# Block-sparse attention and a GELU layer: the selection masks of two more head pairs transposed by DMA

## The chip, the cores and the metric

The kernel runs on one core of a Trainium2 chip. The metric is the device time of one execution in microseconds (us). Times are medians of several runs; the profile shows one execution in detail. The core has a matrix engine (TensorE, PE in the profile, with its weight loads as PEld), a vector engine (VectorE, DVE), a scalar engine (ScalarE, ACT), a general engine (GpSimd, POOL) and SyncE (SP), whose queue issues almost all transfers here. Each engine works through its own instructions in order and waits on semaphores for the others. Transfers run on 16 shared DMA engines.

## The reference

Input q, k and v have 4 batches, 8 heads, 768 positions and 64 columns per head. Keys are averaged over blocks of 64 positions, each query scores the 12 averages, and may look at its three best blocks (among those not in its future) and at its own block. Attention over the allowed, causal positions follows, and its result, 3072 rows of 512, goes through a two-layer network with 2048 inner columns and the tanh form of GELU.

```python
gate_scores = np.einsum('bhsd,bhnd->bhsn', q, k_rep)
gate_scores = np.where(causal, gate_scores, -1000000000.0)
top_idx = np.argsort(gate_scores, axis=-1)[..., -top_k:]
...
scores = np.where(mask, scores, -1000000000.0)
attn = np.exp(scores)
attn = attn / (np.sum(attn, axis=-1, keepdims=True) + 1e-09)
...
h = x @ w_in
g = 0.5 * h * (1.0 + np.tanh(c * (h + 0.044715 * h * h * h)))
return (g @ w_out).astype(np.float32)
```

## The kernel before, in words

Heads are worked on in pairs, 16 in all: pairs 0 to 3 are batch 0 and have steps of their own, pairs 4 to 15 share one set of steps. The whole program is a list of steps, the string ORDER, written out by a planner; `do` takes them one after the other, so an engine's own sequence is the sequence of that engine's steps in the list. A step's name is a letter or two, the pair, and sometimes a part; behind `:` stands the engine that a copy runs on (a ScalarE, v VectorE, p GpSimd), behind `@` which of three PSUM slots ("wide" tiles, two banks each) a product uses.

For a pair p of 4 to 15, in rough order: `d` loads q, k and v (two transfers each, line 422). `hn` and `ln` split q and k into a high and a low 16-bit part (lines 184, 186, 738). `zqh`, `zkh` and `zql` turn them by a DMA transpose on SP (line 750), and `c0`, `c1` copy the halves into the operand tile `qk` (line 757). `s` and `b` make the block sums of the keys on PE (`kp`, line 764) and VectorE, `g` the gate scores on PE (line 793). `m` selects on VectorE: eight-largest search, comparison, and at line 820 the mask `madd16`, laid out by query.

The score product wants the mask by block, as 12 additional rows of `qk` beside the 64 rows of q. So the mask is transposed, and this is where there are two ways. `mt` (line 829) does five 128x128 transposes on PE into the PSUM tile "small", of which there is one for all users: `kp`, `gt`, `mt` and `xt` take it in turn. `zm` (line 839) does one DMA transpose on SP into an SBUF tile that shares two buffers with `zql`. Pairs 4 to 12 use the first, pairs 13 to 15 the second. Either way `mc` (line 845) then copies the two heads' 12 rows into `qk`, on the engine that ORDER names.

`k` are six groups of score products into wide tiles (`st`, line 858), `x` their exponentials on ScalarE (line 874), `a` the causal cut on GpSimd (line 888), `p` the weighted sums of v (`pv`, line 900), `n` the division by the sum on VectorE (lines 672 and 676). `xt`/`xc` (PE and a copy) or `zx` (a DMA transpose, line 909) put the result into `xT`. Batch 0's steps of the same letters have the lines 477, 511, 634 and 661.

The two-layer network runs in 12 chunks of 256 rows, woven between the pairs: `u` are the products with w_in into a wide tile (`hps`, line 966, eight products of 256 columns in each half), `y` the GELU on ScalarE (line 976), `f` the products with w_out (line 1002), `o` the copy to SBUF (line 1015), `w` the store (line 1020). The weights are loaded by `lw` (line 344) into seven buffers shared with other tiles (`w32`) and converted by `cw` (line 353). `dm` are products of zeros that keep PE running in its early waits (line 1041).

Around the change the list holds, for pair 11, `u.4.3.1 mt.11.0 y.5.3`, then `u.4.2.0`, the VectorE copy `mc.11.0.1`, `hn1.12.0`, the ScalarE copy `mc.11.0.0`, `ln1.12.0`; for pair 12, `p.10.0.1 x.11.0.4 mt.12.0 k.11.0.2 mc.12.0.0`, and later `n.10.0` and `mc.12.0.1`, both copies on VectorE.

Of the kernel before, what the change touches and what calls it, by code (L numbers as in the profile page):

```python
# [39 lines left out]
a.1.1.0 xt.1.0 v.0.1.0:a k.0.1.0.1@1 k.0.1.1.1@2 ma.0.1.1 lw.in.3 x.0.1.1.1 xc.1.0:v lw.in.2  # L40
k.0.1.0.0@0 xt.0.0 xc.0.0:v x.0.1.0.1 k.0.1.1.0@2 ma.0.1.0 dm5 cw.in.1:p x.0.1.0.0 u.0.3.0@1
u.0.3.1 r.0.2.0:p x.0.1.1.0 v.0.1.1:v a.0.1.1 a.0.1.0 r.0.2.1:v cw.in.0:v lw.out.1 lw.out.4
d0.0.4.2 r.1.2.0:p d.4.0 p.1.1.0@0 p.1.1.3 p.1.1.1 p.1.1.2 u.0.2.0@2 n.1.1 u.0.2.1 lw.out.0 y.0.3
xt.1.1 p.0.1.0@0 xc.1.1:v p.0.1.2 p.0.1.1 y.0.2 p.0.1.3 u.0.0.0@1 n.0.1 cw.in.2:a d.4.1 u.0.0.1
r.1.2.1:v cw.in.3:a xt.0.1 t2.0.2@2 xc.0.1:v y.0.0 u.1.2.0@0 hn0.4.0:p s.0.2 u.1.2.1 b.0.2 h2.0.2
t2.1.2@1 y.1.2 l.0.2 cw.out.0:p g.0.2 u.1.1.0@0 lw.out.2 cw.out.1:p m.0.2 lw.out.3 u.1.1.1 lw.out.5
d.5.0 s.1.2 cw.out.4:p mt.0.2 u.1.0.0@2 y.1.1 mc.0.2:v lw.out.7 lw.out.6 ln0.4.0:v u.1.0.1 h2.1.2
cw.out.2:v u.0.1.0@0 y.1.0 l.1.2 d.5.1 u.0.1.1 hn1.4.0:v cw.out.3:v u.1.3.0@2 b.1.2 y.0.1 ln1.4.0:v
u.1.3.1 hn0.5.0:p cw.out.5:v k.0.2.0.0@1 y.1.3 zql.4.0 k.0.2.1.0@0 ma.0.2.0 g.1.2 f.0.0.0 m.1.2
x.0.2.0.0 cw.out.6:p k.0.2.0.1@2 f.0.0.1 s.4.0 x.0.2.1.0 k.0.2.1.1@1 b.4.0 zqh.4.0 ma.0.2.1  # L50
ln0.5.0:v mt.1.2 f.0.0.2 x.0.2.1.1 c.ke.0.1:v d0.0.5.2 k.0.2.0.2@0 x.0.2.0.1 k.0.2.1.2@1 cw.out.7:v
ma.0.2.2 d.6.0 hn1.5.0:v x.0.2.1.2 mc.1.2:a k.1.2.1.0@2 zql.5.0 a.0.2.1 x.0.2.0.2 k.1.2.0.0@1
ma.1.2.0 f.0.0.3 c.q0.0 x.1.2.0.0 c0.4.0.1:v a.0.2.0 d0.1.4.2 g.4.0 o.0.0:a v.0.2.0:p x.1.2.1.0
k.1.2.0.2@0 zkh.4.0 m.4.0 k.1.2.1.2@1 ma.1.2.2 f.0.1.0 v.0.2.1:a x.1.2.0.2 d0.1.5.2 p.0.2.0@2
p.0.2.3 ln1.5.0:v p.0.2.2 c0.4.0.0:a mt.4.0 hn0.6.0:v x.1.2.1.2 d.6.1 ln0.6.0:v p.0.2.1 mc.4.0.0:a
k.1.2.1.1@0 v.1.2.0:p n.0.2 k.1.2.0.1@1 zqh.5.0 mc.4.0.1:a ma.1.2.1 f.0.1.1 c.ke.0.0:a c1.4.0.0:p
c.par.1 zkh.5.0 xt.0.2 x.1.2.0.1 c1.4.0.1:p f.0.1.2 xc.0.2:v c.ke.1.0:v c.q0.1 x.1.2.1.1 s.5.0
# [1035 lines left out]
```

## Time and profile before

| what | value |
|---|---|
| median of 3 runs | 269.88 us |
| the runs | 269.58, 269.88, 270.49 us |
| the profiled execution | 269.6 us, of which the profile's span is 267.9 us |
| instructions in the span | 6830 |
| mask transposes on PE (line 829) | 45, in nine pairs |
| mask transposes by DMA (line 839) | 3 |
| packets under 512 bytes | 105008 of 116431 |

The profile is a page and a set of views of one execution, with times counted from the start of the span. A view of the order of time gives the start of an instruction, how long it took, its engine, its line, what it writes and reads, and how many like it follow; in brackets stands the idle time of its engine before it and what ended that. A view of one tile gives all that writes or reads it, with the shortest, median and longest duration. For SP the time of a transfer is that of its issue; how long it took until the data had landed is a line of its own. Matmuls are pipelined, so their durations overlap; the distance between two starts tells what one costs.

### The profile page before, as it was taken

The numbers are of one execution on the slowest core, as the hardware profiler recorded it, in microseconds if no ns is written. First come the engines' busy times: TensorE is split into PE (matmuls) and PEld (weight loads), VectorE is DVE, ScalarE is ACT, GpSimd is POOL, SyncE is SP. The second block draws the span as 40 slices with busy tenths as digits, with TensorE's granted clock in tenths as the row PEclk, the third lists the DMA queues.
The fourth block names the chain that finished last, engine by engine and source line by source line (L and its number), as shares of the span: only waits on it lengthen the run. The fifth ranks groups of instructions, "written<-read, shape, count | busy, mean of one in ns | idle before, by whom it ended". The sixth has DMA issues, their size and how long they took to land.

```text
span 267.9 us, 6830 instructions
## 1 busy us (share of the span) xinstructions
PE 257.9 (96%) x2756; PEld 179.8 (67%) x2756; DVE 140.9 (53%) x441; ACT 194.5 (73%) x221; POOL 98.9 (37%) x166
## 2 busy tenths in 40 slices
PE   8778999999999999999999999999999999999994
PEld 4545898456668667977676656968666877795641
DVE  3667579788878786657564467523633120011111
ACT  2866966999899987949996968889999924351200
POOL 8375553346506737631874153005332200000000
PEclk9999999999999999999999999999999999999999
DMA  8999999999899996898998995397140400031212
GB/s 159 291 302 336 360 269 336 173 192 232 180 190 177 214 187 163 153 231 167 160 184 173 208 183 121 56 167 174 37 113 17 100 0 2 0 117 63 106 69 78
DMA packets 116431, 43.14 MB, mean 161 GB/s; under 512 B 105008, under 2 KB 109360, under 8 KB 116400
## 3 DMA queue, kind: packets, MB, share of 16 engines
q1 hardware_dynamic: 114288, 42.19, 72.3%
q10 hardware_dynamic: 2112, 0.52, 1.1%
q8 instruction: 21, 0.34, 0.6%
q14 instruction: 10, 0.08, 0.1%
HBM read 27.26 MB, written 6.29 MB: 125 GB/s over the span
## 4 chain that ended last, share of the span: by engine, by line
PE 91%; ACT 5%; DVE 2%; issue 1%; POOL 0%; ACTq 0%; DVEq 0%; POOLq 0%
PE hps L966 31%; PE ops L1002 27%; PE st L858 10%; PE pv L900 6%; PE pso L1002 4%; ACT at L634 3%; PE dm L1041 2%; PE w L463 2%; PE pv L661 1%; PE kp L764 1%; PE st L597 1%; PE st L615 1%; PE gt L793 1%; ACT qk L469 1%; PE mt L829 1%
## 5 line engine op out<-in xcount | busy, mean ns | idle before, releaser
L966 PE MATMUL hps<-xT,w_in 128*128 128x256 f16 x768 | 89.9, 272 | 0.0
L1002 PE MATMUL ops<-w_out,gT 128*128 128x512 f16 (+1 forms) x352 | 82.9, 372 | 0.0
L966 PEld LDWEIGHTS <-w_in 128*128 128x128 f16 x768 | 73.9, 98 | 11.6
L976 ACT ACTIVATE gT<-hps 128x1024 f16<-128x1024 f32 x48 | 48.1, 1024 | 37.2 <-PE hps L966 34.6
L874 ACT ACTIVATE at<-st 128x1024 f16<-128x1024 f32 (+1 forms) x72 | 63.0, 917 | 8.6 <-PE st L858 7.6
L1002 PEld LDWEIGHTS <-gT 128*128 128x128 f16 x400 | 37.3, 97 | 37.0 <-issue 0.8
L888 POOL TENSOR_SCALAR_AFFINE_SELECT at<-at 128x256 f16<-128x256 f16 x72 | 30.7, 445 | 76.1 <-ACT at L874 75.8
L858 PE MATMUL st<-qk 76*128 76x128 f16 (+2 forms) x192 | 36.6, 305 | 0.0
L738 DVE SCALAR_TENSOR_TENSOR ln<-io,hn 128x768 f16<-128x768 f32 x24 | 25.9, 1084 | 8.0 <-ACT hn L184 5.7
L634 ACT ACTIVATE at<-st 128x768 f16<-128x768 f32 (+1 forms) x24 | 20.9, 918 | 3.2 <-PE st L615 3.0
L858 PEld LDWEIGHTS <-qk 76*128 76x128 f16 x192 | 16.4, 97 | 9.5 <-issue 0.4
L186 POOL TENSOR_SCALAR hn<-io 128x768 f16<-128x768 f32 x8 | 17.3, 2162 | 10.2 <-DMA io<-in_q_dram 10.1
L1015 DVE COPY osb<-ops 128x512 f32<-128x512 f32 (+1 forms) x11 | 7.2, 652 | 23.4 <-PE ops L1002 23.4
L900 PEld LDWEIGHTS <-at 128*128 128x128 f16 x504 | 17.0, 97 | 1.2
L900 PE MATMUL pv<-v,at 128*128 128x65 f16 x504 | 17.7, 193 | 0.0
L757 POOL COPY qk<-khT 64x768 f16<-64x768 f16 x13 | 13.9, 1074 | 5.7 <-DMA khT<-hn 3.4
L976 ACT ACT_TABLE_LOAD x10 | 12.8, 1283 | 0.2
L1015 DVE COPY w_o<-ops 128x512 f32<-128x512 f32 x3 | 2.1, 692 | 20.1 <-PE ops L1002 20.1
L676 DVE TENSOR_TENSOR xn<-pv,zrec 128x768 f16<-128x768 f32 x12 | 11.5, 958 | 0.4
L672 DVE RECIPROCAL zrec<-pv 128x12 f32<-128x12 f32 x12 | 2.8, 230 | 16.1 <-PE pv L900 16.0
L1015 ACT COPY osb<-ops 128x512 f32<-128x512 f32 x5 | 2.9, 586 | 11.2 <-PE ops L1002 11.2
L1041 PE MATMUL dm<-zsrc 128*128 128x512 f16 (+3 forms) x31 | 9.8, 437 | 1.1 <-POOL zsrc L234 1.1
(150 smaller groups left out, 308.8 us busy)
## 6 DMA issues: line engine op xcount, KB each, us to landing
io<-in_q_dram SPq DMA_DIRECT2D x24, 192.0 KB, 4.4
io<-in_k_dram SPq DMA_DIRECT2D x24, 192.0 KB, 3.8
w_in<-in_moe_w_in_dram SPq DMA_DIRECT2D x8, 512.0 KB, 6.9
w_out<-in_moe_w_out_dram SPq DMA_DIRECT2D x8, 512.0 KB, 7.1
out_dram<-osb SPq DMA_DIRECT2D x15, 256.0 KB, 2.8
w_v<-in_v_dram SPq DMA_DIRECT2D x16, 192.0 KB, 4.2
out_dram<-w_o SPq DMA_DIRECT2D x8, 256.0 KB, 2.2
io<-in_v_dram SPq DMA_DIRECT2D x12, 128.0 KB, 5.7
```

The lines of the kernel that those rows point to most:

```text
L186: math_on[eng].tensor_scalar(out=out, in0=in_, scalar1=c, scalar2=None, op0=ALU.mult)
L634: nc.scalar.activation(out=ov, in_=iv, func=AF.Exp, bias=0.0, scale=SCALE / (QS * QS))
L738: math_on[eng].scalar_tensor_tensor(out=g.rearrange("p t c -> p (t c)"), in0=IO[p, x].rearrange("p t h d -> p (t h d)"), scalar=QS, in1=U[ ...
L757: copy_on[eng](out=dst[0:64, :], in_=U["qh" if x == 0 else "kh", p][64 * hh:64 * hh + 64])
L858: nc.tensor.matmul(st[:, hh, cb:cb + nq * 128], kt[p % 2][hh][0:64 + NBLK, jc * 128:(jc + 1) * 128], qt[p % 2][hh][0:64 + NBLK, qc * 128:( ...
L874: nc.scalar.activation(out=ov, in_=iv, func=AF.Exp, bias=0.0, scale=SCALE / (QS * QS))
L888: nc.gpsimd.affine_select(out=a, in_=a, compare_op=ALU.is_ge, fill=0.0, base=0, pattern=[[0, 2], [1, 128]], channel_multiplier=-1,)
L900: nc.tensor.matmul(U["pv", p][:, o:o + 65], AT[p, hh, jc, qc], v16[p % NSLOT][:, jc, hh, :], start=(jc == 0), stop=(jc == qc),)
L966: nc.tensor.matmul(hps[:, j * TCH:(j + 1) * TCH], w_in16[:, ci, fi * 128:(fi + 1) * 128], xT[:, ci, t0:t0 + TCH], start=(ci == 0), stop=(c ...
L976: nc.scalar.activation(out=g.rearrange("p a w -> p (a w)"), in_=G["h", ch, dj], func=AF.Gelu_apprx_tanh, bias=0.0, scale=1.0,)
L1002: nc.tensor.matmul(G["o", ch, ti][:, a:b], G["g", ch, dj][:, j, row * 128:(row + 1) * 128], w_out16[:, fi, a:b], start=(fi == 0), stop=(fi ...
L1041: nc.tensor.matmul(U["dm"][:, 0:m * 128].rearrange("p (a x) -> p a x", a=m), zsrc, zsrc.unsqueeze(1).to_broadcast([128, m, 128]), start=Tr ...
```

## The change

Two conditions change: pairs 11 and 12 get the step `zm` in place of `mt`. And ORDER is written anew. Taken engine by engine, its sequences are those of before with these exceptions: PE no longer has `mt.11.0` and `mt.12.0`; SP has `zm.11.0` between `w.3.0` and `zkh.12.0`, and `zm.12.0` between `d.15.0` and `zkh.13.0`; on VectorE `mc.11.0.1` comes after `ln1.12.0` and `mc.12.0.0` after `n.10.0`; on ScalarE `mc.11.0.0` comes after `y.4.2`. How the steps of different engines are interleaved in the list differs from the first line on, the wide slots 0 and 1 are exchanged from there on (with `p.1.0.0` and `k.1.1.1.1` taking each the other's slot), and the shared `w32` buffers are asked for by `lw.out.1`, `lw.out.4` and `r.0.2.0`, and by `d.10.2` and `o.3.1`, in another order.

```diff
-        if p in (13, 14, 15):
+        if p in (11, 12, 13, 14, 15):
             step(f"zm.{un}", mask_dma, p)
         else:
             step(f"mt.{un}", mask_t, p)
```

The lines of ORDER around the two masks and the slot exchange:

```diff
-x.1.1.1.0 l.0.1 b.0.1 p.1.0.0@0 p.1.0.1 p.1.0.3 p.1.0.2 x.1.1.0.0 v.0.0.0:v k.1.1.1.1@1 cw.in.4:p
...
-g.11.0 f.4.0.0 w.3.0 m.11.0 x.10.0.2 a.10.0.3 u.4.3.0@0 a.9.0.4 hn1.13.0:p u.4.3.1 mt.11.0 y.5.3
-u.4.2.0@2 mc.11.0.1:v a.9.0.3 hn1.12.0:v u.4.2.1 a.9.0.0 mc.11.0.0:a ln1.12.0:v zkh.12.0 v.10.0:p
...
-p.10.0.1 x.11.0.4 mt.12.0 k.11.0.2@2 mc.12.0.0:v a.11.0.4 f.5.0.0 x.11.0.2 n.10.0 c1.12.0.1:p
-f.5.0.1 a.11.0.5 zx.10.0 mc.12.0.1:v c1.12.0.0:p k.11.0.3@1 ln1.13.0:v f.5.0.2 x.11.0.3 d.14.1
...
+dd.1.2.0 b.0.1 cw.in.4:p x.1.1.0.0 lw.in.1 p.1.0.0@1 p.1.0.1 p.1.0.3 p.1.0.2 lw.in.0 k.1.1.1.1@0
...
+u.4.3.1 zm.11.0 y.5.3 u.4.2.0@2 a.9.0.3 hn1.12.0:v u.4.2.1 a.9.0.0 ln1.12.0:v zkh.12.0 v.10.0:p
+y.4.3 u.5.1.0@0 y.4.2 p.9.0.0@1 d.14.0 v.11.0:p u.5.1.1 c1.11.0.1:p d.13.0 mc.11.0.1:v mc.11.0.0:a
...
+g.12.0 k.11.0.1@2 m.12.0 f.4.1.1 y.5.2 d.15.0 k.11.0.4@0 f.4.1.2 zm.12.0 zkh.13.0 f.4.1.3 x.11.0.1
...
+f.5.0.1 a.11.0.5 mc.12.0.0:v c1.12.0.0:p zx.10.0 mc.12.0.1:v k.11.0.3@0 ln1.13.0:v f.5.0.2 x.11.0.3
```

More of the change, by code (lines that the diff above doesn't have):

```diff
@@ L40 @@
[L40 to L57, printed above, removed]
@@ new lines @@
+cw.in.6:p k.1.1.1.0@0 mt.1.1 dm4 dd.0.2.1 mc.1.1:a s.0.1 cw.in.7:p ma.1.1.0 l.0.1 dm6 x.1.1.1.0
+dd.1.2.0 b.0.1 cw.in.4:p x.1.1.0.0 lw.in.1 p.1.0.0@1 p.1.0.1 p.1.0.3 p.1.0.2 lw.in.0 k.1.1.1.1@0
+v.0.0.0:v dm3 n.1.0 g.0.1 dd.1.2.1 k.1.1.0.1@2 m.0.1 dm3 p.0.0.0@1 p.0.0.2 p.0.0.3 p.0.0.1 lw.in.3
+ma.1.1.1 cw.in.5:p dm4 x.1.1.1.1 dm6 lw.in.2 mt.0.1 x.1.1.0.1 v.1.1.0:p mc.0.1:v n.0.0 lw.out.1
+a.1.1.1 xt.1.0 v.1.1.1:a k.0.1.0.1@0 k.0.1.1.1@2 lw.out.4 a.1.1.0 v.0.1.0:a xc.1.0:v ma.0.1.1
+d0.0.4.2 k.0.1.0.0@1 x.0.1.1.1 xt.0.0 xc.0.0:v x.0.1.0.1 k.0.1.1.0@2 v.0.1.1:v cw.in.1:p d.4.0
@@ new lines @@
+ma.0.1.0 dm5 x.0.1.0.0 u.0.3.0@0 r.0.2.0:p r.0.2.1:v cw.in.0:v x.0.1.1.0 u.0.3.1 a.0.1.1 p.1.1.0@1
+p.1.1.3 a.0.1.0 p.1.1.1 p.1.1.2 u.0.2.0@2 r.1.2.0:p n.1.1 y.0.3 lw.out.0 u.0.2.1 xt.1.1 y.0.2
+p.0.1.0@1 xc.1.1:v p.0.1.2 p.0.1.1 p.0.1.3 u.0.0.0@0 cw.in.2:a n.0.1 u.0.0.1 cw.in.3:a r.1.2.1:v
+d.4.1 xt.0.1 y.0.0 t2.0.2@2 xc.0.1:v u.1.2.0@1 s.0.2 lw.out.2 u.1.2.1 b.0.2 h2.0.2 hn0.4.0:p
+lw.out.3 t2.1.2@0 y.1.2 l.0.2 g.0.2 cw.out.0:p u.1.1.0@1 m.0.2 u.1.1.1 cw.out.1:p lw.out.5 s.1.2
+d.5.0 mt.0.2 u.1.0.0@2 cw.out.4:p y.1.1 mc.0.2:v ln0.4.0:v lw.out.7 u.1.0.1 h2.1.2 lw.out.6
@@ new lines @@
+u.0.1.0@1 cw.out.2:v y.1.0 l.1.2 u.0.1.1 d.5.1 hn1.4.0:v u.1.3.0@2 cw.out.3:v y.0.1 b.1.2 zql.4.0
+u.1.3.1 ln1.4.0:v hn0.5.0:p k.0.2.0.0@0 y.1.3 cw.out.5:v k.0.2.1.0@1 ma.0.2.0 g.1.2 f.0.0.0 m.1.2
+k.0.2.0.1@2 x.0.2.0.0 f.0.0.1 x.0.2.1.0 s.4.0 k.0.2.1.1@0 b.4.0 zqh.4.0 cw.out.6:p ma.0.2.1 mt.1.2
+f.0.0.2 x.0.2.1.1 ln0.5.0:v d0.0.5.2 k.0.2.0.2@1 x.0.2.0.1 k.0.2.1.2@0 d.6.0 ma.0.2.2 c.ke.0.1:v
+x.0.2.1.2 cw.out.7:v k.1.2.1.0@2 mc.1.2:a zql.5.0 hn1.5.0:v k.1.2.0.0@0 a.0.2.1 x.0.2.0.2 ma.1.2.0
+c0.4.0.1:v f.0.0.3 x.1.2.0.0 c.q0.0 d0.1.4.2 a.0.2.0 g.4.0 zkh.4.0 o.0.0:a k.1.2.0.2@1 m.4.0
@@ new lines @@
+k.1.2.1.2@0 v.0.2.0:p x.1.2.1.0 ma.1.2.2 f.0.1.0 d0.1.5.2 v.0.2.1:a x.1.2.0.2 p.0.2.0@2 p.0.2.3
+ln1.5.0:v c0.4.0.0:a p.0.2.2 d.6.1 mt.4.0 p.0.2.1 hn0.6.0:v x.1.2.1.2 k.1.2.1.1@1 v.1.2.0:p
+ln0.6.0:v zqh.5.0 mc.4.0.0:a k.1.2.0.1@0 ma.1.2.1 c1.4.0.0:p f.0.1.1 mc.4.0.1:a n.0.2 zkh.5.0
+c.ke.0.0:a c1.4.0.1:p c.par.1 xt.0.2 f.0.1.2 x.1.2.0.1 xc.0.2:v c.q0.1 c.ke.1.0:v d.7.1 s.5.0
+a.1.2.0 x.1.2.1.1 k.4.0.1@2 b.5.0 v.1.2.1:p k.4.0.0@0 d.4.2 x.4.0.1 hn1.6.0:v k.4.0.2@1 f.0.1.3
+ln1.6.0:v x.4.0.0 p.1.2.0@2 o.0.1:v p.1.2.1 x.4.0.2 a.4.0.0 s.6.0 c1.5.0.0:p w.0.1 k.4.0.3@0 b.6.0
@@ new lines @@
+w.0.0 g.5.0 c0.5.0.1:a k.4.0.4@1 a.4.0.1 zqh.6.0 a.1.2.1 f.1.0.0 x.4.0.3 m.5.0 f.1.0.1 x.4.0.4
+p.1.2.2 zql.6.0 a.4.0.4 k.4.0.5@0 p.1.2.3 x.4.0.5 a.4.0.3 c.ke.1.1:v mt.5.0 f.1.0.2 c1.5.0.1:p
+n.1.2 mc.5.0.1:a zkh.6.0 f.1.0.3 c0.5.0.0:a a.4.0.5 mc.5.0.0:v a.4.0.2 d.7.0 hn1.7.0:v k.5.0.5@1
+k.5.0.0@0 x.5.0.5 v.4.0:v xt.1.2 k.5.0.3@2 x.5.0.0 o.1.0:v d.8.1 p.4.0.0@1 xc.1.2:v c1.6.0.1:p
+x.5.0.3 p.4.0.1 g.6.0 c0.6.0.0:a zkh.7.0 u.2.0.0@0 m.6.0 u.2.0.1 k.5.0.2@2 y.2.0 n.4.0 f.1.1.0
+d.8.0 f.1.1.1 hn0.7.0:v ln0.7.0:v mt.6.0 zqh.7.0 k.5.0.1@0 x.5.0.2 f.1.1.2 c0.6.0.1:v c1.6.0.0:v
@@ new lines @@
+a.6.0.5 k.6.0.0@0 a.6.0.1 g.8.0 a.6.0.2 x.6.0.0 zx.4.0 k.7.0.5@1 k.7.0.0@2 m.8.0 f.2.0.3 x.7.0.5
+a.6.0.0 x.7.0.0 d.9.1 a.6.0.3 k.7.0.1@0 k.7.0.2@1 x.7.0.1 c0.8.0.1:v p.6.0.0@2 d.10.0 c0.8.0.0:v
+p.6.0.1 o.2.0:v a.7.0.1 x.7.0.2 a.7.0.5 mt.8.0 w.1.1 k.7.0.3@0 mc.8.0.0:v f.2.1.0 a.7.0.2 n.6.0
+mc.8.0.1:a f.2.1.1 x.7.0.3 c1.8.0.0:v d.10.1 k.7.0.4@1 c1.8.0.1:v a.7.0.3 xt.6.0 v.7.0:v x.7.0.4
+a.7.0.0 f.2.1.2 xc.6.0:v d.11.0 k.8.0.1@2 a.7.0.4 k.8.0.5@0 hn1.9.0:p p.7.0.0@1 x.8.0.1 p.7.0.1
+x.8.0.5 k.8.0.0@2 n.7.0 k.8.0.2@0 x.8.0.0 a.8.0.1 f.2.1.3 ln0.9.0:v x.8.0.2 a.8.0.0 xt.7.0
@@ new lines @@
+k.8.0.4@1 xc.7.0:v zql.9.0 k.8.0.3@2 o.2.1:v x.8.0.4 u.3.3.0@0 ln1.9.0:v x.8.0.3 u.3.3.1 a.8.0.4
+zkh.9.0 a.8.0.2 u.3.0.0@1 hn1.10.0:a hn0.10.0:p s.9.0 zqh.9.0 u.3.1.0@2 b.9.0 u.3.0.1 y.3.3 d.8.2
+ln1.10.0:v c1.9.0.0:p u.3.1.1 y.3.0 ln0.10.0:v zqh.10.0 u.3.2.0@0 y.3.1 u.3.2.1 c1.9.0.1:v zql.10.0
+g.9.0 y.3.2 u.4.1.0@1 m.9.0 d.11.1 v.8.0:p f.3.0.0 a.8.0.3 w.2.1 u.4.1.1 c0.10.0.0:p d.9.2
+u.5.0.0@2 a.8.0.5 d.12.0 u.5.0.1 mt.9.0 y.5.0 f.3.0.1 mc.9.0.0:v c0.9.0.1:v y.4.1 u.4.0.0@0
+mc.9.0.1:v c0.9.0.0:v u.4.0.1 hn1.11.0:a zkh.10.0 s.10.0 y.4.0 p.8.0.0@2 b.10.0 p.8.0.1 hn0.11.0:v
@@ new lines @@
+k.9.0.3@1 ln0.11.0:v zqh.11.0 g.10.0 f.3.0.2 n.8.0 x.9.0.3 w.2.0 k.9.0.1@0 f.3.0.3 m.10.0 zkh.11.0
+x.9.0.1 k.9.0.5@2 k.9.0.4@1 x.9.0.5 a.9.0.1 k.9.0.2@0 d.13.1 o.3.0:a a.9.0.5 k.9.0.0@2 hn0.12.0:p
+x.9.0.2 f.3.1.0 zql.11.0 mt.10.0 c0.10.0.1:a f.3.1.1 x.9.0.0 d.11.2 v.9.0:p ln0.12.0:v f.3.1.2
+c1.10.0.1:a c1.10.0.0:p u.5.3.0@0 mc.10.0.0:a ln1.11.0:v u.5.3.1 mc.10.0.1:a c1.11.0.0:p zql.12.0
+k.10.0.1@2 x.9.0.4 s.11.0 f.3.1.3 d.12.1 b.11.0 a.9.0.2 x.10.0.1 k.10.0.3@1 o.3.1:a d.10.2
+k.10.0.2@2 x.10.0.3 g.11.0 f.4.0.0 m.11.0 x.10.0.2 w.3.0 a.10.0.3 u.4.3.0@1 a.9.0.4 hn1.13.0:p
@@ new lines @@
+zm.14.0 c0.14.0.1:p u.7.0.1 zkh.14.0 k.13.0.3@0 y.7.0 f.6.0.3 zqh.15.0 y.7.1 p.12.0.0@1 o.6.0:v
+p.12.0.1 v.15.0:a ln1.15.0:v f.6.1.0 c1.14.0.0:p c1.14.0.1:a n.12.0 f.6.1.1 v.13.0:p mc.14.0.1:a
+k.13.0.0@2 s.15.0 k.13.0.5@1 f.6.1.2 b.15.0 x.13.0.3 mc.14.0.0:v f.6.1.3 x.13.0.5 k.14.0.4@0
+x.13.0.0 o.6.1:v k.14.0.3@1 g.15.0 w.6.1 x.14.0.3 u.8.0.0@2 a.13.0.0 zx.12.0 m.15.0 a.13.0.1
+a.13.0.3 x.14.0.4 u.8.0.1 c0.15.0.1:p f.7.0.0 a.14.0.3 a.13.0.5 f.7.0.1 zm.15.0 y.8.0 f.7.0.2
+c1.15.0.0:a f.7.0.3 k.14.0.5@1 k.14.0.1@0 o.7.0:v p.13.0.0@2 w.7.0 x.14.0.5 p.13.0.1 mc.15.0.1:a
@@ new lines @@
+a.14.0.5 k.14.0.2@1 n.13.0 f.7.1.0 mc.15.0.0:a x.14.0.1 f.7.1.1 c0.15.0.0:v v.14.0:v x.14.0.2
+k.14.0.0@2 c1.15.0.1:v f.7.1.2 x.14.0.0 a.14.0.2 k.15.0.1@0 a.14.0.1 f.7.1.3 a.14.0.4 x.15.0.1
+a.14.0.0 k.15.0.2@1 p.14.0.0@2 x.15.0.2 k.15.0.3@0 p.14.0.1 o.7.1:a a.15.0.2 x.15.0.3 k.15.0.0@1
+n.14.0 f.8.0.0 x.15.0.0 k.15.0.4@0 zx.14.0 u.8.2.0@2 a.15.0.0 x.15.0.4 a.15.0.3 k.15.0.5@1 zx.13.0
+u.8.2.1 x.15.0.5 a.15.0.5 u.8.1.0@0 a.15.0.4 w.6.0 a.15.0.1 u.8.1.1 y.8.2 p.15.0.0@1 y.8.1 p.15.0.1
+u.8.3.0@2 n.15.0 u.8.3.1 xt.15.0 y.8.3 f.8.0.1 xc.15.0:v f.8.0.2 f.8.0.3 u.9.1.0@0 o.8.0:a
```

105 lines of the change are left out of this document (32 added, 73 removed).

## The prediction

> **What bounds the kernel now.** I read the page's busy lines first, then the busy time by stretches of 20 us (columns: stretch and length, then busy us and instruction count of PE, PEld, DVE, ACT and POOL, granted clock, DMA share, GB/s).
>
> ```profile
> span 267.9 us, 6830 instructions
> PE 257.9 (96%) x2756; PEld 179.8 (67%) x2756; DVE 140.9 (53%) x441; ACT 194.5 (73%) x221; POOL 98.9 (37%) x166
> PE 91%; ACT 5%; DVE 2%; issue 1%; POOL 0%; ACTq 0%; DVEq 0%; POOLq 0%
> ```
>
> ```profile
> 120.00:140.00 20.00, 20.00 (x218) 14.26 (x216) 13.80 (x45) 19.31 (x23) 11.72 (x13) 1.00 1.04 175
> 140.00:160.00 20.00, 20.00 (x213) 12.75 (x211) 10.12 (x33) 15.13 (x17) 8.28 (x16) 1.00 0.95 184
> ```
>
> The granted clock is 1.00 in both, so no throttle enters the sum. PE is busy 20.00 of 20 us in the two stretches that hold pairs 11 and 12, and the chain that ends last is 91% PE; waits of PE show only near the start (a row at 20.63 us stands further down). So what is taken off PE's queue at 137 or 154 us should come off the end, unless something else then arrives late. Busy time includes pipelined tails, so the saving must be read from start to start. PE in order of time around the two groups of transposes (start, us, engine, line, count):
>
> ```profile
> 135.47 1.91 PE L966 MATMUL hps<-xT,w_in 128*128 128x256 f16 x16
> 137.37 0.45 PE L829 MATMUL mt<-ident,madd 128*128 128x128 f16 x5
> 137.66 2.78 PE L966 MATMUL hps<-xT,w_in 128*128 128x256 f16 x24
> 140.32 0.80 PE L900 MATMUL pv<-v,at 128*128 128x65 f16 x21
> 143.22 0.27 PE L858 MATMUL st<-qk 76*128 76x128 f16 x2
> 152.79 1.45 PE L900 MATMUL pv<-v,at 128*128 128x65 f16 x42
> 154.08 0.44 PE L829 MATMUL mt<-ident,madd 128*128 128x128 f16 x5
> 154.36 0.60 PE L858 MATMUL st<-qk 76*128 76x512 f16 x2
> 159.12 1.03 PE L858 MATMUL st<-qk 76*128 76x256 f16 x6
> ```
>
> **What the change takes off PE.** The 24 products after pair 11's transposes take 140.32 - 137.66 = 2.66 us, 0.111 each; the 16 before them need 1.77 at that pace and have 137.37 - 135.47 = 1.90, so 0.13 us of it is a wait. The transposes themselves move the next start by 137.66 - 137.37 = 0.29. That wait is for the mask itself: VectorE's last selection step starts at 137.09 and takes 0.22 (row below), so it ends at 137.31. Both parts go: 0.42 us. Pair 12's transposes follow 42 products that need 1.29 us from 152.79 to 154.08, with no wait; 154.08 to 154.36 gives 0.28 us. Together 0.70 us. From the far side, ten transposes by their own 219 ns each (row below) would be 2.2 us, but each runs under its neighbours' tails and the starts decide. I take 0.70.
>
> **What the change adds.** Two transposes on SP's queue. They are not a new kind of work: the three for pairs 13 to 15 stand in the trace, and the view of the tile mt between 169 and 200 us shows them with the copies behind them (min/median/max ns); then the same tile between 135 and 160 us, where PE transposes it:
>
> ```profile
> L839 SPq DMA_TRANSPOSE mt<-madd x3: 1200/1210/1212, 170.0 to 196.2; - x3
> L845 DVE COPY qk<-mt x3: 318/319/319, 172.6 to 191.4; 12x640 f16<-12x640 f16 x3
> DMA to landing us min/median/max: 2.6/2.6/2.6
> ```
>
> ```profile
> L829 PE MATMUL mt<-ident,madd x10: 218/219/230, 137.4 to 154.3; 128*128 128x128 f16 x10
> ```
>
> ```profile
> 135.26 0.78 SPq L1020 DMA_DIRECT2D out_dram<-osb  x1
> 139.15 1.22 SPq L750 DMA_TRANSPOSE khT<-hn  x1
> 150.44 1.19 SPq L422 DMA_DIRECT2D io<-in_q_dram  x2
> 151.73 1.54 SPq L750 DMA_TRANSPOSE khT<-hn  x1
> 153.31 1.17 SPq L422 DMA_DIRECT2D io<-in_k_dram  x2
> 156.38 1.23 SPq L909 DMA_TRANSPOSE xT<-xn  x1
> ```
>
> Each occupies SP for 1.21 us and lands 2.6 us after it starts. Pair 11's (zm.11) finds SP with nothing to do from 136.04 to 139.15, so it starts when the mask is ready, at about 137.35, and is off SP at 138.6, ahead of the next step. Pair 12's (zm.12) stands behind the loads that SP issues until 151.63; the mask is ready then, so nothing queued behind it waits for VectorE. It pushes the two issues after it by about 1.25 us, to 154.5 + 1.25 = 155.7, and SP is idle until 156.38 there: the delay is gone before the next step. SP is passed at no cost.
>
> The landings decide. Rows for the same queue: the quiet transpose at 139.15, the loads at 150.44, and the transpose at 151.73 (three views of one tile in one short window each):
>
> ```profile
> DMA to landing us min/median/max: 2.8/2.8/2.8
> ```
>
> ```profile
> DMA to landing us min/median/max: 3.8/3.9/4.0
> ```
>
> ```profile
> DMA to landing us min/median/max: 5.5/5.5/5.5
> ```
>
> zm.11: between 137.35 + 2.6 = 139.95 and 137.35 + 5.5 = 142.85. Only the store of 135.26 was issued in the two us ahead of it, so the queue is nearly as quiet as at 139.15: I take 2.9, about 140.3. zm.12: between 151.65 + 2.6 = 154.25 and 151.65 + 5.5 = 157.15. The load ahead lands at about 151.05 + 4.0 = 155.05, and a transpose needs a little more, so I take 155.7.
>
> **Who waits for the landings.** The copies leave their old places and wait for a DMA instead of PE.
>
> ```profile
> 137.09 0.22 DVE L820 TENSOR_TENSOR madd<-lt,ownm 128x120 f16<-128x120 f16 x1
> 139.04 1.04 DVE L738 SCALAR_TENSOR_TENSOR ln<-io,hn 128x768 f16<-128x768 f32 x1
> 142.68 0.23 DVE L672 RECIPROCAL zrec<-pv 128x12 f32<-128x12 f32 x1 [2.60 <-PE pv L900]
> 156.90 0.96 DVE L738 SCALAR_TENSOR_TENSOR ln<-io,hn 128x768 f16<-128x768 f32 x1
> 157.77 0.35 DVE L757 COPY qk<-qhT 64x768 f16<-64x768 f16 x1
> ```
>
> ```profile
> 138.56 0.68 ACT L845 COPY qk<-mt 12x640 f16<-12x640 f16 x1
> 142.09 1.02 ACT L976 ACTIVATE gT<-hps 128x1024 f16<-128x1024 f32 x1 [0.90 <-PE hps L966]
> ```
>
> Pair 11 on VectorE: the copy now follows the step that ended at 140.08, in a hole of 2.60 us; 140.3 + 0.32 is far from 142.68. On ScalarE the 0.68 us copy moves behind two activations into the 0.90 us hole before the activation at 142.09. Landing at 140.3, it ends by 141.05; the activation, with PE 0.42 earlier, can start at 141.67. It must end before PE's scores of pair 10 at 143.22, 142.80 after the change, whose PSUM slot it empties; 141.67 + 1.02 = 142.69. So the copy costs nothing up to a landing at about 141.0.
>
> Pair 12 on VectorE: the two copies come after the normalisation of pair 10, then the steps shown at 156.90 and 157.77, whose last one PE needs for pair 12's first scores (159.12, 158.42 after the change). Landing at 155.7: copies to 156.4, 0.87 to the next start, 0.35, done at 157.6. That leaves 0.8 us; from a landing at about 156.5 on PE waits. I cost both copies at nothing; uncovered, each us of lateness past those points is a us of PE.
>
> **The rest of the diff.** Read engine by engine, the two lists differ only in these steps; elsewhere the steps are interleaved anew and the names of two PSUM slots are exchanged. One exchange is real: the first weighted sums of pair group 1 take the slot of an earlier transposition instead of that of a score tile.
>
> ```profile
> 20.63 0.53 PE L661 MATMUL pv<-v,at 128*128 128x65 f16 x12 [0.78 <-ACT at L634]
> 22.55 0.53 PE L661 MATMUL pv<-v,at 128*128 128x65 f16 x12
> ```
>
> ```profile
> 19.33 0.68 DVE L477 SCALAR_TENSOR_TENSOR ql<-w,qk 128x512 f16<-128x512 f32 x1
> 21.66 0.69 DVE L676 TENSOR_TENSOR xn_1.0_476<-pv,zrec_1.0_474 128x512 f16<-128x512 f32 x1
> ```
>
> The slot's earlier owner is read out at 19.33 + 0.68 = 20.01, so the sums could start up to 0.58 us before 20.63 (the wait quoted is 0.78). But the next such group, at 22.55, needs VectorE's product that ends at 22.35, and VectorE reaches that product only through its own queue. Between 0 and 0.58 us of gain; I take 0. Besides, the weight and output buffers are asked for in another order at two places, so that a weight load can wait for another cast than before.
>
> ```profile
> 38.78 3.01 POOL L353 CAST w_out<-w_out 128x1024 f16<-128x1024 f32 x3
> w_out<-in_moe_w_out_dram SPq DMA_DIRECT2D x8, 512.0 KB, 7.1
> ```
>
> Casts are 3.01 / 3 = 1.0 us apart, so a load can start 1.0 us later or earlier. It lands 7.1 us after its issue, behind others: the start is hidden by that backlog, and I take 0 between -1.0 and +1.0.
>
> Sum: 269.6 - 0.70 = 268.90 for the profiled execution, which lies 0.28 below the median of 269.88; as a median 269.18.
>
> The Trainium skill (VectorE: DVE Perf Modes, "Rules for kernel authors") speaks against the change: it says to transpose 128x128 on TensorE where PSUM will do as destination, and to take the DMA crossbar otherwise. This case's trace agrees in latency, 0.45 us against 2.6, and by that rule TensorE should keep the masks: the time would be that of the second rival below, 271.0 against 269.18.
>
> **The rivals.** First, the start does gain: with the whole 0.58, 269.18 - 0.58 = 268.60. For it speaks the idle 0.78 us at 20.63; against it the VectorE row at 21.66. Second, the slower one: zm.11 lands late and ScalarE stands at its copy. From a landing at 141.0 on, the activation behind it is late, PE's scores of pair 10 wait for the slot, and at the upper end, 142.85, the price is 1.85 us: 269.18 + 1.85 = 271.0. For it speaks the DMA share of 1.04 in that stretch and the 5.5 us row; against it SP's empty stretch before 139.15 and the 2.8 us row behind it. Third, zm.12 lands like the 5.5 us row that stands in its place now, at 157.15: copies and two steps end at 159.1, PE waits 0.7 us, and the gain is gone, 269.85. Fourth, the change removes PE work that some other engine would have held up anyway, so that the time stays at 269.9; 20.00 busy us of 20 speak against it.
>
> **How the numbers follow.** A measurement of this kernel tells about 0.3% (0.8 us) from no change. Forecast 0.48, start gains 0.17, late pair 11 0.19, late pair 12 0.11, nothing 0.05. The forecast lies at that line: 0.70 under the median, and 0.98 under it if the profiled execution's own 268.90 is the typical one; so I put 0.28 of its 0.48 beyond and 0.20 within. Faster 0.28 + 0.17 = 0.45; of late pair 12, 0.08 within and 0.03 past it, since its landing has no firm upper end: same 0.20 + 0.08 + 0.05 = 0.33; slower 0.19 + 0.03 = 0.22. The range goes up to the forecast with its loads 1.0 late, 270.2, and 0.2 more for the late tail of pair 12, 270.4, which takes in the third and fourth rival and leaves out the second; down to the first rival less the 0.3 us by which the fastest run shown (269.58) lies under the median, 268.3. Some 0.2 is left outside.
>
> **What would show it.** Right: 35 products at line 829 and five transposes at 839; PE still 20.00 of 20 around 140 and 160; the steps after 160 us 0.7 earlier; landings near 2.9 and 4.0 us. Wrong: idle ScalarE time before a copy at line 845 followed by PE scores waiting for an activation; VectorE idle before 845 past 156.5; PE at 24 us earlier than now; a span that shrinks by over 1 us or grows.

## The result, and the profile after

| | before | after |
|---|---|---|
| median of five runs each, taken together | 270.31 us | 271.77 us |
| lowest to highest | 269.58 to 270.49 us | 271.61 to 272.97 us |
| ratio after to before | | 1.0076, 95% interval 1.0051 to 1.0102 |
| profiled execution, its span | 269.6, 267.9 us | 272.97, 271.2 us |

The changed kernel is slower by 0.5 to 1.0%, about 2 us; 271.77 lies past the upper end of the range, 270.4. The profiled execution of the changed kernel is the slowest of its five, so sums on the profiles are made against their own difference, 271.2 - 267.9 = 3.3 us.

The head of the page of after, and its chain of waits by engine:

```profile
span 271.2 us, 6816 instructions
PE 258.4 (95%) x2746; PEld 179.4 (66%) x2746; DVE 140.3 (52%) x441; ACT 194.7 (72%) x221; POOL 99.5 (37%) x166
PE 84%; DVE 6%; DMA 4%; SPq 2%; ACT 1%; issue 1%; POOL 0%; DVEq 0%; POOLq 0%
```

Ten matmuls fewer were recorded, as the change says, and yet PE's share of the chain fell from 91% to 84%; transfers, which had no share before, have 4%. Where PE stands is read from the busy time by stretches (columns as in the prediction), after first, then the rows of before that were not shown:

```profile
40.00:60.00 20.00, 18.68 (x253) 12.37 (x251) 14.13 (x45) 16.54 (x20) 9.13 (x10) 1.00 0.96 225
60.00:80.00 20.00, 17.77 (x231) 11.22 (x227) 16.10 (x54) 16.39 (x21) 9.36 (x17) 1.00 0.98 196
...
120.00:140.00 20.00, 20.00 (x215) 14.11 (x214) 12.53 (x45) 17.36 (x21) 8.67 (x11) 1.00 1.05 189
140.00:160.00 20.00, 20.00 (x220) 13.73 (x218) 10.28 (x31) 16.14 (x18) 9.55 (x15) 1.00 1.05 190
160.00:180.00 20.00, 19.29 (x207) 14.39 (x206) 11.86 (x34) 15.65 (x19) 4.97 (x7) 1.00 0.68 133
```

```profile
40.00:60.00 20.00, 19.26 (x264) 12.58 (x263) 16.92 (x48) 17.36 (x22) 8.29 (x11) 1.00 1.15 235
60.00:80.00 20.00, 19.94 (x236) 12.85 (x235) 17.17 (x56) 18.54 (x22) 8.58 (x17) 1.00 1.05 201
```

The clock is 1.00 throughout. The stretches that hold the two masks, 120 to 160 us, are as full as the prediction said. The time was lost 80 us ahead of the first mask: 0.58 + 2.17 = 2.75 us of PE between 40 and 80 us. A smaller piece, 0.71 us, is missing after 160. The view of PE's waits between 54 and 76 us in after, its three longest rows (who waits for whom: us in total, times, longest); before has no row in that view:

```profile
PE xt_0.2_1319 L689 <- DVE xn_0.2_1312 L676: 0.9, 1, 0.9
PE mt L829 <- DVE madd L820: 0.7, 1, 0.7
PE gt L793 <- DMA qhT<-hn: 0.6, 1, 0.6
```

The earliest of these waits in time is for a transfer, the transposed `qhT` of pair 4 at 56.07 us; VectorE, for which PE waits next, itself stood three times for the loads of q and k in that stretch. So transfers are late, and SP's queue tells since when. SP in order of time, before and then after (start, us on SP, line, transfer, how many follow):

```profile
34.61 1.70 SPq L422 DMA_DIRECT2D io<-in_k_dram  x2
36.40 3.82 SPq L344 DMA_DIRECT2D w_out<-in_moe_w_out_dram  x3
40.27 1.05 SPq L422 DMA_DIRECT2D io<-in_q_dram  x2
...
44.85 5.22 SPq L750 DMA_TRANSPOSE qlT<-ln  x1
50.12 1.28 SPq L750 DMA_TRANSPOSE qhT<-hn  x1
```

```profile
35.49 1.18 SPq L422 DMA_DIRECT2D io<-in_k_dram  x2
40.74 1.39 SPq L344 DMA_DIRECT2D w_out<-in_moe_w_out_dram  x3
42.19 1.12 SPq L422 DMA_DIRECT2D io<-in_q_dram  x2
...
48.14 4.94 SPq L750 DMA_TRANSPOSE qlT<-ln  x1
53.12 1.28 SPq L750 DMA_TRANSPOSE qhT<-hn  x1
```

The three weight loads are `lw.out.2`, `lw.out.3` and `lw.out.5`. The first of them starts at 36.40 before and at 40.74 after; SP issues nothing from 35.49 + 1.18 = 36.67 to 40.74, that is for 4.07 us. What it waits for, and where that stands on GpSimd (two rows of SP's waits, then GpSimd in order of time, both of after):

```profile
SPq L344 <- DMA w_out<-in_moe_w_out_dram: 2.2, 1, 2.2
SPq L344 <- POOL w_out L353: 1.8, 1, 1.8
```

```profile
37.59 2.13 POOL L186 TENSOR_SCALAR hn<-io 128x768 f16<-128x768 f32 x1 [5.81 <-DMA io<-in_q_dram]
39.68 3.73 POOL L353 CAST w_out<-w_out 128x1024 f16<-128x1024 f32 x3
```

The first of these casts is `cw.out.0`. In the two built programs the tile of `lw.out.2` lies in different buffers of the seven: before in the one that held `lw.in.2`, cast long ago; after in the one that holds `lw.out.0`, whose cast runs from 39.68 to about 40.7. So SP first waits 2.2 us for `lw.out.0` to land and then 1.8 us for its cast. Before, SP waits for that cast too, but only with the third load of the group, when the first two, 1 MB, are on their way. The DMA engines meanwhile ran out of work. Busy time by shorter stretches, before and then after (the last two columns are the DMA share and GB/s):

```profile
36.00:41.00 5.00, 5.00 (x61) 4.63 (x60) 3.98 (x16) 2.27 (x3) 4.30 (x4) 1.00 1.11 327
41.00:46.00 5.00, 5.00 (x47) 4.30 (x45) 4.93 (x10) 3.69 (x4) 0.84 (x2) 1.00 1.10 320
```

```profile
36.00:41.00 5.00, 5.00 (x62) 4.63 (x60) 3.48 (x15) 2.11 (x4) 3.41 (x3) 1.00 0.74 191
41.00:46.00 5.00, 5.00 (x49) 4.44 (x46) 3.23 (x6) 3.84 (x4) 2.41 (x2) 1.00 0.74 275
```

5 x (327 - 191) + 5 x (320 - 275) = 905, that is 0.9 MB not moved by 46 us, or 2.8 us at the 320 GB/s of before. The trace has `zql.4.0` landing at 55.05 instead of 52.06 and `zqh.4.0` at 56.03 instead of 53.02: 3.0 us late each, and PE's gate scores of pair 4 start 0.04 us behind the second.

Now the masks themselves, the view of the tile `mt` from 138 to 165 us in after:

```profile
L839 SPq DMA_TRANSPOSE mt<-madd x2: 1207/1350/1492, 140.7 to 155.0; - x2
...
DMA to landing us min/median/max: 3.0/4.0/5.1
```

Pair 11's landed in 3.0 us, pair 12's in 5.1. ScalarE around pair 11's copy, then VectorE and PE around pair 12's, all in order of time:

```profile
141.80 1.94 ACT L976 ACTIVATE gT<-hps 128x1024 f16<-128x1024 f32 x2
143.79 0.72 ACT L845 COPY qk<-mt 12x640 f16<-12x640 f16 x1
144.98 1.02 ACT L976 ACTIVATE gT<-hps 128x1024 f16<-128x1024 f32 x1 [0.46 <-PE hps L966]
```

```profile
160.20 0.67 DVE L845 COPY qk<-mt 12x640 f16<-12x640 f16 x2 [1.81 <-DMA mt<-madd]
160.90 1.17 DVE L738 SCALAR_TENSOR_TENSOR ln<-io,hn 128x768 f16<-128x768 f32 x1
162.00 0.55 DVE L757 COPY qk<-qhT 64x768 f16<-64x768 f16 x1
```

```profile
160.86 1.03 PE L1002 MATMUL ops<-w_out,gT 128*128 128x512 f16 x4
162.60 1.03 PE L858 MATMUL st<-qk 76*128 76x256 f16 x6 [0.71 <-DVE qk L757]
```

Pair 11's copy sits between two activations, and the second of them still waits 0.46 us for PE: it costs nothing. Pair 12's copies wait 1.81 us for their landing; two steps of VectorE later PE has waited 0.71 us for pair 12's first scores.

### The profile page after: what moved, and what is told of

Read it like the earlier page. It is cut to its first block, busy times and chain, and to the rows that moved or that the text cites. A ratio compares the mean times of both kernels' runs of the same rounds, so it can differ in the third digit from the quotient of the medians.

```text
span 271.2 us, 6816 instructions
## 1 busy us (share of the span) xinstructions
PE 258.4 (95%) x2746; PEld 179.4 (66%) x2746; DVE 140.3 (52%) x441; ACT 194.7 (72%) x221; POOL 99.5 (37%) x166
## 4 chain that ended last, share of the span: by engine, by line
PE 84%; DVE 6%; DMA 4%; SPq 2%; ACT 1%; issue 1%; POOL 0%; DVEq 0%; POOLq 0%
PE hps L966 31%; PE ops L1002 23%; PE st L858 9%; PE pv L900 5%; PE pso L1002 4%; PE dm L1041 2%; PE w L463 2%; DMA mt<-madd 2%; DMA io<-in_k_dram 1%; PE pv L661 1%; PE st L597 1%; DMA qhT<-hn 1%; PE gt L793 1%; PE kp L764 1%; PE st L615 1%
## 5 line engine op out<-in xcount | busy, mean ns | idle before, releaser
L858 PE MATMUL st<-qk 76*128 76x128 f16 (+2 forms) x192 | 36.7, 305 | 0.9 <-DVE qk L757 0.7
L858 PEld LDWEIGHTS <-qk 76*128 76x128 f16 x192 | 16.2, 97 | 10.8 <-issue 1.2
L1002 PE MATMUL pso<-w_out,gT 128*128 128x512 f16 (+1 forms) x48 | 10.5, 361 | 0.0
```

The lines of the kernel that those rows point to most:

```text
L858: nc.tensor.matmul(st[:, hh, cb:cb + nq * 128], kt[p % 2][hh][0:64 + NBLK, jc * 128:(jc + 1) * 128], qt[p % 2][hh][0:64 + NBLK, qc * 128:( ...
L1002: nc.tensor.matmul(G["o", ch, ti][:, a:b], G["g", ch, dj][:, j, row * 128:(row + 1) * 128], w_out16[:, fi, a:b], start=(fi == 0), stop=(fi ...
```

## The experiments

Theory 1: the new order of the list gave `lw.out.2` a buffer with a late cast, the DMA engines fell behind near 40 us, and PE paid for it between 55 and 73 us. Theory 2: the exchange of the wide slots costs it. Theory 3: the two transposes by DMA cost it, by holding SP, VectorE or a transfer. In all kernels below ORDER is one line shorter, so their line numbers are one lower (L838 for L839, L857 for L858). All compute the whole reference. Before was run beside them, 269.83 us as the median of 25 runs with `mask_only`, `reorder_only`, `buffers_only` and `mask_d15`, 269.86 us of 35 with the others.

One table serves all of them. It gives, for one PE instruction near each of these times of before, its start in each kernel's profile less its start in before's, in us. A step between two columns is what PE lost or won there.

```
time in before    17.6   25.6   54.1   58.1   62.2   70.3  135.0  139.1  153.0  156.0  159.4  240.5
after            +0.30  +0.15  +0.31  +1.10  +2.01  +3.36  +3.37  +2.93  +2.89  +2.61  +3.48  +3.47
mask_only        -0.23  -0.23  -0.23  -0.23  +0.08  -0.10  -0.11  -0.55  -0.60  -0.88  -0.31  -0.32
reorder_only     +0.57  +0.42  +0.42  +0.80  +2.39  +2.49  +2.91  +2.90  +2.90  +2.90  +2.90  +2.89
buffers_only     -0.15  -0.14  +0.28  +0.28  +1.11  +0.93  +0.93  +0.93  +0.92  +0.92  +0.92  +0.92
mask_d15         +0.69  +0.69  +0.69  +0.69  +1.22  +1.03  +1.02  +0.58  +0.53  +0.25  +0.25  +0.25
after_healed     -0.24  -0.28  -0.28  -0.28  -0.46  -0.30  -0.31  -0.75  -0.80  -1.08  -0.61  -0.62
after_d15        -0.17  -0.27  -0.19  +0.54  +1.51  +1.34  +1.32  +0.88  +0.84  +0.56  +0.56  +0.74
slots_only       -0.21  -0.68  -0.68  -0.68  -0.78  -0.69  -0.70  -0.71  -0.70  -0.70  -0.70  -0.71
mask_d15_slot    -0.20  -0.67  -0.67  -0.20  +0.53  +0.62  +1.30  +0.85  +0.81  +0.53  +0.53  +0.69
```

**The masks alone** (`mask_only`): the list of before, with only the mask steps and their copies moved as in the change.

```diff
-u.4.3.1 mt.11.0 y.5.3 u.4.2.0@2 mc.11.0.1:v a.9.0.3 hn1.12.0:v u.4.2.1 a.9.0.0 mc.11.0.0:a ln1.12.0:v
+u.4.3.1 zm.11.0 y.5.3 u.4.2.0@2 a.9.0.3 hn1.12.0:v u.4.2.1 a.9.0.0 ln1.12.0:v
...
-y.4.2 p.9.0.0@0
+y.4.2 mc.11.0.0:a p.9.0.0@0
...
-a.10.0.1 n.9.0
+a.10.0.1 mc.11.0.1:v n.9.0
...
-d.15.0 y.5.2
+d.15.0 zm.12.0 y.5.2
...
-mt.12.0 k.11.0.2@2 mc.12.0.0:v a.11.0.4 f.5.0.0 x.11.0.2 n.10.0
+k.11.0.2@2 a.11.0.4 f.5.0.0 x.11.0.2 n.10.0 mc.12.0.0:v
```

> The step list of before with nothing changed but the masks of pairs 11 and 12 (the two DMA transposes, their copies moved as in the change). Theory 1, that the loss is a weight buffer given to the wrong load near 40 us: PE runs as before up to 137 us and then gains 0.42 and 0.28 us; 0.7 us faster than before, 269.6, or 269.6 plus up to 0.9 if the mask of pair 12 again lands late. Theory 2, that the exchange of two PSUM slots near 20 us is the loss: the same time. Theory 3, that the DMA transposes are the loss: slower than before by 1 us or more.

Measured 269.17 us (12 runs), ratio 0.9974 (0.9954 to 0.9994): faster than before by 0.26%. In the table PE wins 0.44 us between 135 and 139 and 0.28 between 153 and 156, and loses 0.57 at 159. Theory 3 falls. Pair 12's lateness is real, though; the tile `mt` from 149 to 165 us, the two lines on its transfer, and PE's waits from 150 to 165:

```profile
L838 SPq DMA_TRANSPOSE mt<-madd x1: 1206/1206/1206, 151.5 to 151.5; - x1
...
DMA to landing us min/median/max: 5.0/5.0/5.0
```

```profile
PE st L857 <- DVE qk L756: 0.4, 1, 0.4
```

**The new list without the masks** (`reorder_only`): the changed list with both masks on PE again, their copies in the places of before.

```diff
-u.4.3.1 zm.11.0 y.5.3 u.4.2.0@2 a.9.0.3 hn1.12.0:v
+u.4.3.1 mt.11.0 y.5.3 u.4.2.0@2 a.9.0.3 mc.11.0.1:v hn1.12.0:v
...
-f.4.1.2 zm.12.0 zkh.13.0
+f.4.1.2 zkh.13.0
...
-p.10.0.1 k.11.0.2@2
+p.10.0.1 mt.12.0 k.11.0.2@2
```

> The changed step list with the PE transposes of pairs 11 and 12 put back where they were, so each engine has the sequence of before. Theory 1 and theory 2: slower than before by what the change lost at its start, 2 to 3.4 us, 272.3 to 273.7, with the third load of w_out issued near 40.7 instead of 36.4 us (theory 1). Theory 3: the time of before, 270.3.

Measured 272.47 us (6 runs), ratio 1.007 (1.0044 to 1.0097). The loss of the median is there without the change that the diff is named after; in the profile PE loses 2.07 us between 54 and 70. The three loads start at 39.63 (40.7 expected). PE's longest wait from 54 to 76 us is the one that is longest in after, and at the same instruction; in `mask_only` it is 0.3 us:

```profile
PE xt_0.2_1319 L688 <- DVE xn_0.2_1312 L675: 1.9, 1, 1.9
```

**Two requests moved** (`buffers_only`): the list of before with `lw.out.1` and `lw.out.4` ahead of `r.0.2.0`. No engine's own sequence changes by it, only the order in which tiles ask for the seven buffers; in the built program `lw.out.2` then has the buffer of `lw.out.0`, as in after.

```diff
-u.0.3.1 r.0.2.0:p x.0.1.1.0 v.0.1.1:v a.0.1.1 a.0.1.0 r.0.2.1:v cw.in.0:v lw.out.1 lw.out.4 d0.0.4.2
+u.0.3.1 lw.out.1 lw.out.4 r.0.2.0:p x.0.1.1.0 v.0.1.1:v a.0.1.1 a.0.1.0 r.0.2.1:v cw.in.0:v d0.0.4.2
```

> The step list of before; two weight loads (lw.out.1 and lw.out.4) stand ahead of the copy r.0.2.0 in the list, as in the change; no engine's own sequence changes, only which of the seven shared buffers each tile gets. Theory 1: the third load of w_out waits for a cast that ends near 39.8 and goes out near 40 instead of 36.4 us, and the time rises by 1.5 to 3 us. Theories 2 and 3: the time of before within 0.3 us.

Measured 272.35 us (8 runs, 270.47 to 274.48), ratio 1.009 (1.0059 to 1.012). SP in order of time:

```profile
34.72 1.59 SPq L421 DMA_DIRECT2D io<-in_k_dram  x1
39.54 1.86 SPq L343 DMA_DIRECT2D w_out<-in_moe_w_out_dram  x3
```

The loads wait until 39.54 (36.40 before), and by the medians two names moved in a list cost as much as the whole change, as theory 1 said. Not all of that is seen as a wait. The profile is of one of the two runs with a granted clock of 1.000, 270.52 us, and PE loses 0.92 us in it; the other such run took 270.47. The three runs at a mean granted clock of 0.985 to 0.994 took 272.0 to 274.5 us, the three at 0.997 and 0.998 272.2 to 273.1. By an estimate from these figures, 1.5% less clock is 4 us of 270, as much as the longest run has over the shortest; 0.2 to 0.3% is under 1 us and doesn't explain the last three.

**The changed kernel with the old start** (`after_healed`): before's list up to `zql.4.0` with the wide slots exchanged, then the changed list. `lw.out.2` has the buffer of `lw.in.2` again.

```diff
-u.0.3.0@0 r.0.2.0:p r.0.2.1:v cw.in.0:v x.0.1.1.0 u.0.3.1 a.0.1.1 p.1.1.0@1
+u.0.3.0@0 u.0.3.1 r.0.2.0:p x.0.1.1.0 v.0.1.1:v a.0.1.1 a.0.1.0 r.0.2.1:v cw.in.0:v lw.out.1 lw.out.4
...
-u.1.2.0@1 s.0.2 lw.out.2 u.1.2.1
+u.1.2.0@1 hn0.4.0:p s.0.2 u.1.2.1
...
-l.0.2 g.0.2 cw.out.0:p u.1.1.0@1 m.0.2 u.1.1.1 cw.out.1:p lw.out.5
+l.0.2 cw.out.0:p g.0.2 u.1.1.0@1 lw.out.2 cw.out.1:p m.0.2 lw.out.3 u.1.1.1 lw.out.5
```

> The changed kernel with the start of its list (up to zql.4.0) in the order of before and with the wide slots exchanged as the change has them; everything behind it is the changed list. The output load lw.out.2 gets the buffer of lw.in.2 again, as before. Theory 1 (the buffer with the late cast): lw.out.2 is issued by 37 us, the PE stalls of 0.80, 1.10 and 0.86 us near 56, 63 and 72 us are gone, pair 12's stall near 160 us stays (0.5 to 0.9), and the time is about 269.2, ratio 0.996 to 0.998. Rival (the rest of the interleaving, the wide slots or the masks cost the time): the time stays near 271.8, ratio 1.007.

Measured 269.59 us (12 runs), ratio 0.9981 (0.9959 to 1.0003), against 1.0076 for the change. Its SP queue and its busy time by stretches:

```profile
34.53 2.03 SPq L421 DMA_DIRECT2D io<-in_k_dram  x2
36.65 3.50 SPq L343 DMA_DIRECT2D w_out<-in_moe_w_out_dram  x3
```

```profile
40.00:60.00 20.00, 19.26 (x264) 12.47 (x262) 16.38 (x48) 17.64 (x22) 7.98 (x10) 1.00 1.14 235
60.00:80.00 20.00, 19.98 (x236) 12.76 (x235) 17.55 (x56) 18.53 (x23) 9.57 (x18) 1.00 1.17 203
```

The loads start at 36.65 again, PE is as full as before, and the table shows nothing lost from 54 to 70 us. As built, this kernel and the changed one have the same sequence on every engine and differ only in the buffers of 16 tiles, all among the seven. With theory 1's cause taken out of the changed kernel, its loss is gone; only pair 12's 0.47 us at 159 stays. The median is 0.4 above the 269.2 expected, the ratio just past the upper end of the expected 0.998.

**Pair 12's place on SP** (`mask_d15`, `after_d15`): the loads `d.15.0` issued behind `zkh.13.0` instead of ahead of `zm.12.0`, once in `mask_only`, once in the changed kernel, whose diff is shown.

```diff
-d.15.0 k.11.0.4@0 f.4.1.2 zm.12.0 zkh.13.0
+k.11.0.4@0 f.4.1.2 zm.12.0 zkh.13.0 d.15.0
```

> mask_only with the load d.15.0 behind the transposes zm.12.0 and zkh.13.0 on SP, so that pair 12's mask goes out with a shorter queue ahead of it. Theory 1: the mask lands about 3 us after its issue, PE has no wait at pair 12's first scores, and the time is 269.6 at most, no slower than mask_only. If pair 12's landing was on time in mask_only already: the same as mask_only. Theory 3: as slow as mask_only.

> The changed kernel with the two loads d.15.0 issued behind zkh.13.0, so that zm.12.0 is no longer behind them. If the loads ahead of it make zm.12 late: zm.12 lands within 4 us of its issue and before 158, PE's stall of 0.87 us at 162.6 is gone, the stalls before 75 us stay, and the time is 271.77 less 0.6 to 0.9, about 271.0 (ratio 1.004). Rival (the instruction fetch or the queue state alone makes it late, or PE waits for something else there): a stall of 0.5 us or more stays near 160, and the time is that of the change, ratio 1.007.

`mask_d15` measured 269.05 us (12 runs), ratio 0.997 (0.9953 to 0.9987); `after_d15` 271.09 us (12 runs, 270.13 to 274.73), ratio 1.0063 (1.0027 to 1.0098; it leaves out the longest run). In both the table has 0.00 between 156 and 159, where `mask_only` lost 0.57 and after 0.87. The transfer of the tile `mt` in `after_d15`:

```profile
L838 SPq DMA_TRANSPOSE mt<-madd x1: 1200/1200/1200, 152.5 to 152.5; - x1
...
DMA to landing us min/median/max: 2.6/2.6/2.6
```

The landing takes 2.6 us instead of 5.0 to 5.2, and PE's waits from 150 to 165 us have no row left. By the traces the move is worth 0.5 to 0.9 us; in the times the intervals of `mask_d15` and `mask_only` overlap, as do those of `after_d15` and after, so the gain is not shown there. What widens `after_d15` is the clock again: its seven runs at 0.999 or 1.000 took 270.1 to 271.4 us, all below the five of after (271.6 to 273.0, at 0.998 or more), and its five at 0.987 to 0.994 took 273.2 to 274.7.

**The wide slots** (`slots_only`, and `mask_d15_slot`, which is `mask_d15` with the exchange).

```diff
-x.1.1.1.0 l.0.1 b.0.1 p.1.0.0@0 p.1.0.1
+x.1.1.1.0 l.0.1 b.0.1 p.1.0.0@1 p.1.0.1
...
-v.0.0.0:v k.1.1.1.1@1
+v.0.0.0:v k.1.1.1.1@0
```

> The kernel before, with wide slots 0 and 1 exchanged from the first weighted sums of pair group 1 on, as the change has it; no other step moves, and the w32 buffers are those of before. Theory 1: p.1.0.0 starts 0.3 to 0.6 us earlier at 20 us and loses it by 25 us; the time is that of before within 0.3%, 269.6 to 270.4. Rival 2 (the exchange costs the time): ratio 1.007 with the stalls near 56, 63 and 72 us. Rival 1 of the prediction (the start gains): 269.3, ratio 0.998.

> The list of before with the two masks by DMA, d.15.0 behind zkh.13.0 and the wide slots exchanged: the version that should hold all that gains. If the slot exchange is worth nothing: that of the same version without the exchange, 269.05, ratio 0.997. If the start gains its 0.3 to 0.5 us: 268.6, ratio 0.995. If the exchange costs: over 269.5.

`slots_only` measured 269.90 us (12 runs), ratio 0.9984 (0.9965 to 1.0003); `mask_d15_slot` 269.22 us (12 runs), 0.9973 (0.9953 to 0.9994). Theory 2 falls: the exchange costs nothing. The first weighted sums of pair group 1, and the next such group, in `slots_only` (20.63 and 22.55 before):

```profile
19.95 0.53 PE L660 MATMUL pv<-v,at 128*128 128x65 f16 x12 [0.31 <-DVE kbd L495]
21.87 0.53 PE L660 MATMUL pv<-v,at 128*128 128x65 f16 x12
```

PE wins 0.47 us here in every profile with the exchange (0.68 - 0.21 for `slots_only` in the table), and contrary to what I expected `slots_only` keeps it to the end, as `mask_d15_slot` does to 54; after, `reorder_only`, `after_healed` and `after_d15` lose 0.32 to 0.43 of it again by 25.6. No interval shows a gain. `mask_d15_slot` is no better than `mask_d15`, and its profile, with `lw.out.2` in the old buffer, still lost 1.29 us from 54 to 70: there the three loads started at 37.67, with PE 0.67 us ahead of before, so 1.9 us late counted from where PE stands. So these loads cost PE time when another cause makes them late, too. The size doesn't follow the start alone: from 54 to 70 `buffers_only`, at 39.54, lost 0.65 us and `reorder_only`, at 39.63, 2.07; no run shows why. Of the kernels run, `mask_d15` has the lowest median, 269.05, and beats before; that it beats `mask_only` isn't shown.

## Why the prediction was wrong

**What was right.** The sum's main terms. Predicted 0.42 us off PE at pair 11 and 0.28 at pair 12: the table has 0.44 or 0.45 in all six kernels with the masks on DMA (135 to 139), and 0.28 in all six at pair 12 (153 to 156). The masks alone measured 0.26% under before, 0.7 us; that this is the predicted 0.70 is partly luck, since in that kernel's profile they won 0.72 us and lost 0.57 at 159, and the interval, 0.06 to 0.46%, reaches down to 0.16 us, about the 0.15 left. Pair 11's mask behaved as written: 3.0 us to landing against the 2.9 taken, its ScalarE copy in the hole ahead of an activation, no wait. SP was passed at no cost to the steps named. The second rival, a late pair 11, did not happen; the 271.0 that it gave stands near the measured time by accident.

**The step that failed** is the last term of the rest of the diff: "It lands 7.1 us after its issue, behind others: the start is hidden by that backlog, and I take 0 between -1.0 and +1.0." The mechanism was named and put at nothing, and three things in that were wrong. First, the size: a cast later was put at 1.0 us, since casts follow each other by 1.0. But the new buffer's cast did not follow another; it was the first, behind a 2.13 us split on GpSimd that itself waited for a load, and SP stood 4.07 us until that buffer's load had landed and been cast. Second, the backlog: it didn't hide the later start, it ran out. The rate from 36 to 41 us was 191 GB/s instead of 327, and the two transposes of pair 4 landed 3.0 us later. Third, what is behind the waiting instruction: the prediction priced the weight load, while SP's queue holds the loads of pair 5 and the transposes of pair 4 behind it, and PE waits for those, in part through VectorE. Within the changed kernel the term was +3.05 us (54 to 70), and taking its cause out brings the ratio from 1.0076 to 0.9981.

**The third rival happened, and in full.** Pair 12 landed in 5.1 us, as the 5.5 us row had warned, past the point from which PE was to wait: PE waited, by the table 0.87 us. The forecast's 4.0 us landing, from the load ahead, was wrong in all three kernels that kept the loads ahead of it (5.0, 5.1, 5.2). The price given, 0.7 us of gain lost, was near the 0.87, 0.57 and 0.47 seen. Sum on the profiles: +3.37 by 135 us, less 0.44, 0.04 and 0.28, plus 0.87 makes +3.48; the span grew by 3.3.

**The start, first rival.** The exchange won 0.47 of the 0.58 us allowed, for the stated reason, the earlier slot. The prediction's doubt, that the next group would give it back, was right for after (0.32 of it) and wrong for `slots_only`; why they differ stays open.

**The rule of the Trainium skill** (VectorE: DVE Perf Modes, "Rules for kernel authors") that speaks for TensorE where PSUM will do is not borne out as a rule for time here: with nothing else changed, the transposes by DMA gave a ratio of 0.9974 (0.9954 to 0.9994), although each takes 2.6 to 5.0 us to land against 0.45 on PE.

**Open.** Why the granted clock falls in some runs of the kernels with the late load (below), and why PE's loss from 54 to 70 us lies between 0.65 and 2.07 us in two kernels whose loads start within 0.1 us of each other. And whether the loads ahead or an instruction packet (below) made pair 12 late: moving the loads changed both.
